# First chunk of an mLSTM cell with a feed-forward block: two pairs of up-blocks run in two halves of the batches, with attention of the other batches between them

## The chip, the cores and the metric

The kernel runs on one core of a Trainium2 chip. The metric is the device time of one launch in microseconds (us). The engines are named as in the profile: PE is TensorE (matmuls; PEld its weight loads), DVE is VectorE, ACT is ScalarE, POOL is GpSimd, SP is the engine whose queue issues all DMAs here.

## The reference

An mLSTM cell (batch 4, 8 heads, 768 steps, head size 40) is followed by a feed-forward block on 3072 tokens of width 320, with a hidden width of 2048.

```python
for t in range(S):
    m_new = np.maximum(f_gate[:, :, t] + m, i_gate[:, :, t])
    f_stab = np.exp(f_gate[:, :, t] + m - m_new)
    i_stab = np.exp(i_gate[:, :, t] - m_new)
    C = f_stab * C + i_stab * outer(v_t, k_t)      # per batch and head, 40x40
    n = f_stab * n + i_stab * k_t
    y[:, :, t] = sigmoid(o_gate[:, :, t]) * (C @ q_t) / np.maximum(np.abs(n @ q_t), 1.0)
...
x = y.transpose(0, 2, 1, 3).reshape(B * S, H * D)  # 3072 x 320
h = x @ w_in                                       # 320 x 2048
out = (h * sigmoid(1.702 * h)) @ w_out             # 2048 x 320
```

All of it is float32.

## The kernel before, in words

The 768 steps are worked off in six chunks (`w`) of 128. In a chunk the recurrence is written as masked attention, batch by batch (`b` = 0 to 3, eight heads each), plus, from the second chunk on, a term from the carried state. The functions that follow are named with their lines in the kernel before.

- `gates(w)` (L226): scans over the gates on DVE, which give the running maximum and what the decay weights need. For the first chunk POOL and DVE split the values into three bf16 parts; for later chunks the running maximum is stored to DRAM (`m_row`, L256) and `spread(w)` (L297) loads it back as a broadcast into `wt`.
- `transposes(w, b)` (L284): k and q with the head size on the partitions. In the first chunk PE does it (L294, eight matmuls a batch) and ACT copies the result (L295); later DVE does it (L288) out of `k_bl` and `q_bl`, which `load_blocks` fills. In the first chunk the tile `q_bl` holds q itself, under the name `q_st`.
- `weights(w, b)` (L304): the decay weights `wt`, in the first chunk by sixteen matmuls (L312, L313) and an Exp on ACT (L314), then a causal mask by a select on POOL (L321).
- `scores(w, b)` (L326): sixteen small matmuls (L331), multiplied with `wt` on DVE (L333).
- `values(w, b)` (L335): 32 small matmuls (L342) and a chain on DVE (L356 to L362) with the sigmoid of the output gate (written with Tanh) and the normalisation, which gives `y`; POOL copies 64 columns of it (L364).
- `seam(w, b)` (L366): three transposes of `y` on PE (L371), copied by ACT into `xT` (L372), the input of the feed-forward block, 512 columns wide: 128 for each batch.
- `up(w, j)` (L397): two pairs of up-blocks, that is, 4 x 128 hidden units. `full` (L407) multiplies the first 256 rows of `w_in`, `rest` (L413) the last 64; then GELU on ACT (L418). `down` (L429) multiplies with `w_out`.
- `carry(w, b)` (L374): the update of the carried state (POOL L378, PE L383, DVE L392 or L394).
- `convert(n)` (L212): the weights come as raw bits, in twenty pieces of 512 KB; each piece is worked over by two ACT instructions (L216, L217) and four DVE instructions (L218 to L223). Pieces 0 and 1 hold the rows 0 to 255 of `w_in` for the first four up-blocks, piece 2 the last 64 rows for the first eight (`w_in_x`), 3 and 4 the next four, and so on; pieces 10 to 19 are `w_out`. `fetch(n)` (L150) loads a piece. Pieces 0 to 5 lie in the six buffers of the pool `sp`, which pieces 10 to 15 use next; so the load of piece 10 waits for the conversion of piece 0, and so on to 15 and 5. The table `beside` says which pieces are converted and fetched with which pair of up-blocks, or down-block.
- `keep_busy(n)` (L174): n matmuls on a tile of zeros, 128x512 in bf16, whose result nobody reads (L176).

The order of the work is written out by hand: every engine executes its instructions in the order in which the program emits them, and waits, instruction by instruction, for the semaphores of what it needs. A PSUM pool of four buffers, `ps_a`, serves transposes, weights, scores, values and seam in turn; a second of four, `ps_m`, serves the up- and down-blocks (and the filler matmuls).

In the first chunk (L533 to L555) the order before is: `gates(0)` and `gates(1)`; then for each batch the transposes, the scores of the batch before it, the weights; pieces 0 and 1 are converted on the way; then POOL clears `state`, `q_bl` and `k_bl` (L541 to L543), and `columns(0)`, the values and the seams of the four batches follow, with fillers between. Only then does the loop over up-blocks start (L569), each block 512 columns wide. After the first pair of blocks come the load of the next output gate, `spread(1)` and `load_blocks(1)` (L580).

Of the kernel before, what the change touches and what calls it, by code (L numbers as in the profile page):

```python
# [8 lines left out]
FP = mybir.dt.float32  # L9
U32 = mybir.dt.uint32  # L10
BF = mybir.dt.bfloat16
AF = mybir.ActivationFunctionType
# [22 lines left out]
def kernel(  # L35
# [13 lines left out]
    B, H, S, D = q.shape  # L49
# [36 lines left out]
    eo = {}  # L86
# [4 lines left out]
    def load_gates(w):  # L91
        for dst, src in ((f_sb, f_gate), (i_sb, i_gate)):
            dst[w] = ld.tile([BH, L], FP, tag="fi", bufs=4, name="fi")
            nc.sync.dma_start(out=dst[w], in_=src[:, :, w * L:(w + 1) * L].rearrange("b h s -> (b h) s"))
# [7 lines left out]
            nc.sync.dma_start(out=dst[:, hs, 0:D],  # L102
                              in_=src[bs, :, w * L:(w + 1) * L, :].rearrange("b h s d -> s (b h) d"))

    def load_blocks(w):
        for dst, src in ((k_bl, k), (q_bl, q)):
            for two in range(2):
                for d in range(0, D, 32):
                    n = min(32, D - d)
                    r = two * 64 + d  # L110
                    for g in range(L // 32):
                        t = w * L + g * 32
                        nc.sync.dma_start(
                            out=dst[r:r + 32, :, g, 0:n],
                            in_=src[:, two:H:2, t:t + 32, d:d + n].rearrange("b j s d -> s (b j) d"))
# [34 lines left out]
    def fetch(n):  # L150
        pool = gp if 6 <= n < 10 else sp
        bits[n] = pool.tile([128, 512, 2], U32, tag="g", name="bits")
        for r, c, src in pieces[n][1]:
            nc.sync.dma_start(out=bits[n][r, c].rearrange("p a two -> p (a two)"), in_=src)

    load_gates(0)
    for b in range(B):
        load(0, "kq", slice(b, b + 1))
        if b == 1:
            load_gates(1)  # L160
        if 0 < b < 3:
            fetch(b - 1)
    for b in range(B):
        load(0, "vo", slice(b, b + 1))
    for n in range(2, 6):
        fetch(n)


# [5 lines left out]
    def keep_busy(n):  # L174
        for _ in range(n):
            T.matmul(p_idle, idle, idle.unsqueeze(1).to_broadcast([128, 4, 128]), start=True, stop=True)  # L176
# [217 lines left out]
                V.tensor_copy(out=state[r, ps, i, :], in_=pc[r])  # L394


    def up(w, j):  # L397


        x = xT[w].rearrange("p c b t -> p c (b t)")  # L400
        ph = {}

        def full(j, first):
            for c in range(2):
                for i in range(2):
                    f = 2 * j + i
                    T.matmul(ph[j][i], w_in_sb[:, c, f * 128:(f + 1) * 128], x[:, c, :], start=(first and c == 0),  # L407
                             stop=(not first and c == 1))

        def rest(j, first):  # L410
            for i in range(2):
                r = slice(i * 64, i * 64 + 64)
                T.matmul(ph[j][i], w_in_x[r, j, :], x[r, 2, :], start=first, stop=not first)  # L413

        def gelu(j):
            g = gs[w, j] = gp.tile([128, 2, W], FP, tag="g", name="g")
            for i in range(2):
                A.activation(out=g[:, i, :], in_=ph[j][i], func=AF.Gelu_apprx_sigmoid)  # L418

        for j, first in ((j, True), (j + 1, False)):  # L420
            ph[j] = [ps_m.tile([128, W], FP, tag="m", name="p_h") for _ in range(2)]
            if first:
                full(j, True)
            rest(j, not first)
            if not first:
                full(j, False)
            gelu(j)
# [94 lines left out]
            f(*args)  # L522


    gates(0)
    gates(1)
    for n in range(6, 10):
        fetch(n)
    for b in range(B + 1):
        if b < B:  # L530
            transposes(0, b)
        if b:
            scores(0, b - 1)  # L533
        if b < B:
            weights(0, b)
        if b:
            keep_busy(2)
        if 0 < b < 3:
            convert(b - 1)
    G.memset(v_st[:, :, D:D1], 1.0)  # L540
    G.memset(state, 0.0)  # L541
    G.memset(q_bl, 0.0)  # L542
    G.memset(k_bl, 0.0)  # L543
    columns(0)
    for b in range(B + 1):
        if b < B:
            hs = slice(b * H, (b + 1) * H)
            A.activation(out=eo[0][:, hs, :], in_=eo[0][:, hs, :], func=AF.Tanh, scale=0.5)
            values(0, b)
            keep_busy(2)  # L550
        else:
            keep_busy(3)
        if b:
            seam(0, b - 1)
    keep_busy(3)  # L555
    convert(2)


    beside = {0: ((3, 4, 5), range(10, 16)), 1: ((6, 7, 8), ()), 2: ((9, 10, 11), (16, 17)), 3: ((12, 13, 14), (18, 19)),
              4: ((15, 16), ()), 9: ((17,), ()), 12: ((18,), ()), 14: ((19,), ())}  # L560

    def weights_in(n):
# [6 lines left out]
    for w in range(NW):  # L569
        more = w + 1 < NW  # L570
        for j in range(NF // 2):
            if j % 2 == 0:
                if w == 0:
                    weights_in(j // 2)
                up(w, j)
            if j == 0 and more:
                load(w + 1, "o")
            if w == 0 and j == 0:
                spread(1)
                load_blocks(1)  # L580
            if w == 1 and j == 1:
                weight_sums()
            if more:
                if w and j == 0:
                    gates(w + 1)
                if j == 4:
                    load(w + 1, "v")
                if w and j == 4:
                    spread(w + 1)
                if j == 4:  # L590
                    load(w + 1, "k")
                if j < B:
                    carry(w, j)
                if 4 <= j < 6 if w else j == 7:
                    first = 2 * j - 8 if w else 0
                    transposes(w + 1, first)
                    transposes(w + 1, first + 1)
            if w and j >= 4:
                hidden_sums(w, (j - 4,), False)
                if j % 2:  # L600
                    hidden_sums(w, (j - 5, j - 4), True)
        side = attention(w + 1) if more else []
        if w == 0:

            blocks = [(lambda b=b, n=n: down(w, b, n)) for ns in ((0, 1), (2,), (3,)) for b in range(B) for n in ns]
            stops = (0, 1, 4, 7, 9, 11, 13, 15)
        else:
            blocks = down_fast(w, 0) + down_fast(w, 1)
            stops = (0, 1, 2, 4, 6, 8, 10, 12)
        for i, block in enumerate(blocks):  # L610
            if w == 0:
                weights_in(4 + i)
                if i in (6, 9):
                    transposes(1, i // 3)
            if w + 2 < NW and i == (0 if w else 9):
                load_gates(w + 2)
                load_blocks(w + 2)
            block()
            if i in stops and side:
                run(side.pop(0))  # L620
# [30 lines left out]
```

## Time and profile before

| | us |
|---|---|
| median of 9 runs | 524.09 |
| lowest, highest | 522.28, 526.94 |
| the profiled execution's own time | 524.12 |
| its span, first to last instruction | 522.4 |

| in the profiled execution | us after the start of the span |
|---|---|
| first transposes on PE | 5.13 |
| first up-block starts | 36.13 |
| first two pairs of up-blocks done, state update starts | 45.31 |
| first down-block starts | 74.05 |
| second chunk's first up-block starts | 123.11 |

A line of a timeline shows the start, the duration (for merged lines from the first start to the last end), the engine, the line of the kernel, the operation, the tiles (out <- in), the shape, the count, and in brackets the time that the engine had been idle before and who ended the wait. PE's records overlap, since matmuls are pipelined: two successive starts, not the durations, give the pace. The page gives busy shares, the chain of work that ended last, and the costliest groups.

### The profile page before, as it was taken

The numbers are of one execution on the slowest core, as the hardware profiler recorded it, in microseconds if no ns is written. First come the engines' busy times: TensorE is split into PE (matmuls) and PEld (weight loads), VectorE is DVE, ScalarE is ACT, GpSimd is POOL, SyncE is SP. The second block draws the span as 40 slices with busy tenths as digits, with TensorE's granted clock in tenths as the row PEclk, the third lists the DMA queues.
The fourth block names the chain that finished last, engine by engine and source line by source line (L and its number), as shares of the span: only waits on it lengthen the run. The fifth ranks groups of instructions, "written<-read, shape, count | busy, mean of one in ns | idle before, by whom it ended". The sixth has DMA issues, their size and how long they took to land.

```text
span 522.4 us, 9549 instructions
## 1 busy us (share of the span) xinstructions
PE 514.6 (98%) x3828; PEld 353.1 (68%) x3828; DVE 267.1 (51%) x603; ACT 169.0 (32%) x367; POOL 70.1 (13%) x104
## 2 busy tenths in 40 slices
PE   8999999999999999999999999999999999999997
PEld 5764447774447998445999544999643799744797
DVE  7769755874675454146445226564217455203511
ACT  3557456612223520322720212630221450032100
POOL 4341000112500212200112100020220021000000
PEclk9999999999999999999999999999999999999999
DMA  9979979267396200596300496500376000000000
GB/s 165 148 246 313 220 76 198 69 76 127 50 230 73 30 14 27 85 231 73 30 26 1 78 243 68 56 28 1 78 163 99 0 28 1 26 0 1 1 26 25
DMA packets 175884, 44.81 MB, mean 86 GB/s; under 512 B 164544, under 2 KB 170720, under 8 KB 175840
## 3 DMA queue, kind: packets, MB, share of 16 engines
q1 hardware_dynamic: 175840, 44.21, 44.8%
q8 instruction: 30, 0.49, 0.4%
q14 instruction: 14, 0.11, 0.1%
HBM read 40.17 MB, written 4.01 MB: 85 GB/s over the span
## 4 chain that ended last, share of the span: by engine, by line
PE 95%; POOL 2%; issue 1%; DVE 1%; ACT 0%; POOLq 0%; DVEq 0%
PE p_h L407 33%; PE p_out L488 30%; PE p_h L413 9%; PE p_out L434 7%; PE p_s L331 5%; PE p_o L342 4%; PE p_i L348 2%; PE p_x L371 1%; PE p_c L383 1%; PE p_t L294 1%; PE p_w L313 0%; PE p_w L312 0%; PE p_idle L176 0%; POOL q_bl L542 0%; POOL k_bl L543 0%
## 5 line engine op out<-in xcount | busy, mean ns | idle before, releaser
L407 PE MATMUL p_h<-xT,w_in_sb 128*128 128x512 f32 x384 | 175.1, 602 | 0.6 <-ACT xT L372 0.6
L407 PEld LDWEIGHTS p_h<-xT,w_in_sb 128*128 128x128 f32 x384 | 69.8, 190 | 92.6 <-issue 89.7
L418 ACT ACTIVATE g<-p_h 128x512 f32<-128x512 f32 x96 | 54.6, 596 | 135.4 <-PE p_h L413 73.5
L488 PE MATMUL p_out<-w_out_sb,g 128*128 128x160 f32 x480 | 71.3, 302 | 0.0
L488 PEld LDWEIGHTS p_out<-w_out_sb,g 128*128 128x128 f32 x480 | 66.8, 190 | 3.7 <-issue 2.4
L493 DVE TENSOR_TENSOR o_sb<-o_sb,p_out 128x160 f32<-128x160 f32 x70 | 21.4, 318 | 65.1 <-PE p_out L488 64.9
L321 POOL TENSOR_SCALAR_AFFINE_SELECT wt<-wt 128x1024 f32<-128x1024 f32 x24 | 26.2, 1093 | 199.7 <-ACT wt L318 186.9
L372 ACT COPY xT<-p_x 128x384 f32<-128x384 f32 x24 | 11.5, 479 | 120.5 <-PE p_x L371 120.5
L413 PE MATMUL p_h<-xT,w_in_x 64*128 64x512 f32 x192 | 48.4, 616 | 0.7 <-ACT g L418 0.7
L318 ACT ACTIVATE wt<-wt,cols 128x128 f32<-128x128 f32 x160 | 48.4, 392 | 0.0
L488 PE MATMUL p_out<-t,s 128*128 128x160 f32 x320 | 47.5, 301 | 0.0
L488 PEld LDWEIGHTS p_out<-t,s 128*128 128x128 f32 x320 | 44.3, 190 | 0.6
L472 DVE TENSOR_TENSOR s<-g 128x512 f32<-128x512 f32 x20 | 13.9, 693 | 54.0 <-ACT g L418 53.6
L333 DVE TENSOR_TENSOR wt<-p_s,wt 128x512 f32<-128x512 f32 x48 | 30.8, 684 | 17.1 <-POOL wt L321 14.9
L392 DVE TENSOR_TENSOR state<-p_c,state 40x164 f32<-40x164 f32 x32 | 10.4, 326 | 55.9 <-PE p_c L383 55.5
L413 PEld LDWEIGHTS p_h<-xT,w_in_x 64*128 64x128 f32 x192 | 16.7, 186 | 30.7 <-issue 27.3
L434 PE MATMUL p_out<-w_out_sb,g 128*128 128x320 f32 x128 | 36.2, 437 | 0.0
L434 PEld LDWEIGHTS p_out<-w_out_sb,g 128*128 128x128 f32 x128 | 23.8, 190 | 10.1 <-issue 0.5
L331 PE MATMUL p_s<-qT,kT 40*128 40x128 f32 x384 | 28.8, 291 | 0.9 <-DVE wt L333 0.9
L342 PEld LDWEIGHTS p_o<-v_st,wt 128*64 128x64 f32 x768 | 24.3, 138 | 4.6 <-issue 3.9
L331 PEld LDWEIGHTS p_s<-qT,kT 40*128 40x128 f32 x384 | 24.1, 193 | 4.6 <-DVE wt L333 1.4
L342 PE MATMUL p_o<-v_st,wt 128*64 128x41 f32 x768 | 27.2, 231 | 0.0
(114 smaller groups left out, 519.2 us busy)
## 6 DMA issues: line engine op xcount, KB each, us to landing
wt<-m_row SPq DMA_DIRECT2D x20, 512.0 KB, 6.8
bits<-in_moe_w_in_dram SPq DMA_DIRECT2D x8, 512.0 KB, 5.9
out_dram<-o_sb SPq DMA_DIRECT2D x24, 160.0 KB, 1.8
eo<-in_o_gate_dram SPq DMA_DIRECT2D x5, 640.0 KB, 5.4
v_st<-in_v_dram SPq DMA_DIRECT2D x5, 640.0 KB, 5.7
k_st<-in_k_dram SPq DMA_DIRECT2D x5, 640.0 KB, 8.4
bits<-in_moe_w_out_dram SPq DMA_DIRECT2D x8, 320.0 KB, 4.6
k_bl<-in_k_dram SPq DMA_DIRECT2D x40, 64.0 KB, 2.6
```

The costliest lines, as they stand in the source:

```text
L318: A.activation(out=x[:, h, :], in_=x[:, h, :], func=AF.Exp, scale=-1.0, bias=cols[w][:, b * H + h:b * H + h + 1])
L321: G.affine_select(out=x, in_=x, compare_op=OP.is_ge, fill=0.0, base=0, pattern=[[0, H], [1, L]], channel_multiplier=-1)
L331: T.matmul(pw[i][:, p, :], kT[w, b][r, p, :], qT[w, b][r, p, :], start=True, stop=True)
L333: V.tensor_tensor(out=wt[w, b][:, :, i, :], in0=pw[i], in1=wt[w, b][:, :, i, :], op=OP.mult)
L342: T.matmul(po[t, h, :], wt[w, b][:, p, i, t], v_st[:, b * H + h, :], start=True, stop=True)
L407: T.matmul(ph[j][i], w_in_sb[:, c, f * 128:(f + 1) * 128], x[:, c, :], start=(first and c == 0), stop=(not first and c == 1))
L413: T.matmul(ph[j][i], w_in_x[r, j, :], x[r, 2, :], start=first, stop=not first)
L418: A.activation(out=g[:, i, :], in_=ph[j][i], func=AF.Gelu_apprx_sigmoid)
L434: T.matmul(po, gs[w, f // 2][:, f % 2, b * L:(b + 1) * L], w_out_sb[:, f, :], start=(f == 0), stop=(f == NF - 1))
L472: V.tensor_tensor(out=s1, in0=a10, in1=a11, op=OP.add)
L488: T.matmul(po, a(f), b[:, f, :], start=(f == 0), stop=(f == NH - 1))
L493: V.tensor_tensor(out=dst, in0=x, in1=po, op=OP.add)
```

## The change

The first chunk gets another order. The loads are issued in the order in which the new order uses them: k and q of batches 0 and 1, the first weight piece, v and the output gate of batch 0, k and q of batch 2, and so on; the second chunk's gates are loaded after the first six pieces. Attention of the first two batches is finished first (their values and seams are run between transposes, scores and weights of batches 2 and 3). Then `up(0, 0)` takes a new argument: it allocates all four PSUM tiles of its two pairs, works on the columns of batches 0 and 1 (256 of 512), and between the parts of this half calls, in this order, scores of batch 3 and values of batch 2; values of batch 3; the seams of batches 2 and 3 and the conversion of pieces 3 and 4. Then the second half, the columns of batches 2 and 3, follows. The Tanh of the output gate becomes a function, `gate_out`. `gates(1)` runs after `up(0, 0)` and the conversion of piece 5, and `load_blocks(1)` is split in two, k before `spread(1)` and q after it. The three big clears of POOL are emitted after the weights of batch 3. Sixteen filler matmuls are left of thirty. The diff, without the parts that only rename:

```diff
-    load_gates(0)
-    for b in range(B):
-        load(0, "kq", slice(b, b + 1))
-        if b == 1:
-            load_gates(1)
-        if 0 < b < 3:
-            fetch(b - 1)
-    for b in range(B):
-        load(0, "vo", slice(b, b + 1))
-    for n in range(2, 6):
-        fetch(n)
+    load_gates(0)
+    for what, n in (("kq", 0), ("kq", 1), (fetch, 0), ("vo", 0), ("kq", 2), ("vo", 1), (fetch, 1), ("kq", 3), (fetch, 2),
+                    ("vo", 2), ("vo", 3), (fetch, 3), (fetch, 4), (fetch, 5)):
+        if what is fetch:
+            fetch(n)
+        else:
+            load(0, what, slice(n, n + 1))
+    load_gates(1)
+    for n in range(6, 10):
+        fetch(n)
...
+        if between:
+            for k in (j, j + 1):
+                ph[k] = [ps_m.tile([128, W], FP, tag="m", name="p_h") for _ in range(2)]
+            ts = slice(0, W // 2)
+            full(j, True)
+            between[0]()
+            rest(j, False)
+            rest(j + 1, True)
+            between[1]()
+            full(j + 1, False)
+            between[2]()
+            ts = slice(W // 2, W)
...
     gates(0)
-    gates(1)
-    for n in range(6, 10):
-        fetch(n)
-    for b in range(B + 1):
-        if b < B:
-            transposes(0, b)
-        if b:
-            scores(0, b - 1)
-        if b < B:
-            weights(0, b)
-        if b:
-            keep_busy(2)
-        if 0 < b < 3:
-            convert(b - 1)
-    G.memset(v_st[:, :, D:D1], 1.0)
+    transposes(0, 0)
+    weights(0, 0)
+    transposes(0, 1)
+    scores(0, 0)
+    weights(0, 1)
+    keep_busy(2)
+    convert(0)
+    scores(0, 1)
+    keep_busy(2)
+    gate_out(0)
+    transposes(0, 2)
+    values(0, 0)
+    weights(0, 2)
+    keep_busy(2)
+    gate_out(1)
+    convert(1)
+    values(0, 1)
+    scores(0, 2)
+    seam(0, 0)
+    transposes(0, 3)
+    weights(0, 3)
     G.memset(state, 0.0)
     G.memset(q_bl, 0.0)
     G.memset(k_bl, 0.0)
+    keep_busy(2)
+    seam(0, 1)
     columns(0)
-    for b in range(B + 1):
-        if b < B:
-            hs = slice(b * H, (b + 1) * H)
-            A.activation(out=eo[0][:, hs, :], in_=eo[0][:, hs, :], func=AF.Tanh, scale=0.5)
-            values(0, b)
-            keep_busy(2)
-        else:
-            keep_busy(3)
-        if b:
-            seam(0, b - 1)
-    keep_busy(3)
     convert(2)
+    gate_out(2)
+    gate_out(3)
...
-    beside = {0: ((3, 4, 5), range(10, 16)), ...
+    beside = {0: ((5,), range(10, 16)), ...
...
-                if w == 0:
-                    weights_in(j // 2)
-                up(w, j)
+                if w == 0 and j == 0:
+                    up(w, j, (lambda: (scores(0, 3), values(0, 2)), lambda: values(0, 3),
+                              lambda: (seam(0, 2), seam(0, 3), convert(3), convert(4))))
+                    weights_in(0)
+                else:
+                    if w == 0:
+                        weights_in(j // 2)
+                    up(w, j)
...
             if w == 0 and j == 0:
+                gates(1)
+                load_blocks(1, 0)
                 spread(1)
-                load_blocks(1)
+                load_blocks(1, 1)
```

The memset of the ones in `v_st` moves ahead of `gates(0)`.

## The prediction

> **What bounds the kernel now.** I read the page first (busy shares and the chain that ended last), then PE's timeline for the first 80 us, then those of DVE, ACT, POOL and the SP queue over the same stretch.
>
> ```profile
> PE 514.6 (98%) x3828; PEld 353.1 (68%) x3828; DVE 267.1 (51%) x603; ACT 169.0 (32%) x367; POOL 70.1 (13%) x104
> ...
> PE 95%; POOL 2%; issue 1%; DVE 1%; ACT 0%; POOLq 0%; DVEq 0%
> ```
>
> TensorE (PE) is the bound: 95% of the chain. The change touches only the first chunk, so the question is by how much PE reaches the end of the first two pairs of up-blocks (the L407 and L413 matmuls up to 45.31 us) earlier or later; whatever PE gains or loses there is carried to the end, provided DVE and the loads keep step.
>
> ```profile
> 22.96 0.60 PE L176 MATMUL p_idle<-idle 128*128 128x512 bf16 x2
> 24.44 1.16 PE L331 MATMUL p_s<-qT,kT 40*128 40x128 f32 x16 [0.88 <-DVE wt L333]
> ...
> 36.13 3.70 PE L407 MATMUL p_h<-xT,w_in_sb 128*128 128x512 f32 x8
> 39.76 1.99 PE L413 MATMUL p_h<-xT,w_in_x 64*128 64x512 f32 x8
> 41.68 3.70 PE L407 MATMUL p_h<-xT,w_in_sb 128*128 128x512 f32 x8
> 45.31 0.81 PE L383 MATMUL p_c<-vw,k_st 128*40 128x41 f32 x32
> ```
>
> The reader should see that both pairs take 45.31 - 36.13 = 9.2 us, that they begin only when all four batches' attention is done, and that PE waits little before (0.88 us here). Much of PE's time before 36 us is filler: the L176 matmuls.
>
> POOL matters too, because of what DVE does while POOL runs. Two places, the second as pieces of the chain:
>
> ```profile
> 1.31 0.74 POOL L199 MEMSET k_st<- 128x768 f32 x1
> 1.41 1.72 DVE L189 TENSOR_SCALAR pick<-ident 32x32 bf16<-32x32 f32 x3 [0.40 <-POOL ident masks.py:199]
> ...
> 1.99 0.74 POOL L199 MEMSET q_bl<- 128x768 f32 x1
> ```
>
> ```profile
> 1.41 1.35 DVE pick L189
> 2.77 0.17 DVE pick L189
> ```
>
> Equal instructions: the first takes 1.35 us, the next 0.17, and the first ends at 2.76, where POOL's two memsets end (1.99 + 0.74 = 2.73). DVE did not get in between the two memsets. The same with a select:
>
> ```profile
> 16.42 0.84 DVE L218 TENSOR_SCALAR w_in_sb<-w_in_sb 128x512 f32<-128x512 f32 x1 [1.66 <-ACT w_in_sb L216]
> ...
> 36.68 0.43 DVE L218 TENSOR_SCALAR w_in_x<-w_in_x 128x512 f32<-128x512 f32 x1 [1.86 <-ACT w_in_x L216]
> 37.14 0.43 DVE L219 TENSOR_SCALAR w_in_x<-w_in_x 128x512 uint32<-128x512 uint32 x1
> ```
>
> L218 needs 0.43 alone, and 0.84 when it starts inside POOL's select of 15.89 to 16.98. The memsets that the change moves (with one of `state`, 1.1 us, ahead of them):
>
> ```profile
> 26.10 1.81 POOL L542 MEMSET q_bl<- 128x2048 f32 x1
> 27.84 1.80 POOL L543 MEMSET k_bl<- 128x2048 f32 x1
> ```
>
> They follow each other without a gap, straight after the last select.
>
> [...] L189 and L218 (tensor_scalar) are held, while L356 to L360, which read PSUM, keep their 0.17 to 0.44 us during the memsets of 25 to 29.6 us. [...] Here 16 p_s take 2.08 us at 11.28 and 1.16 at 17.49, so the clock rose near 17 us in this execution; no fall is seen after it.
>
> **The change, step by step.** Letters per batch: T = eight L294, W = sixteen L312/L313, S = scores L331, V = values L342, X = seam L371. Prices at full clock from the timelines: PE T 1.0, W 0.9, S 1.09, V 1.06, X 0.33, two fillers 0.45. DVE: product after S 1.25 (L333 twice), chain after V 1.48 (27.33 to 28.81; p_o is free after 0.96), one convert 2.36 (36.68 to 39.04). ACT: copy 0.5 to 0.6, Exp 0.55, each half of a convert 0.57 (DVE can start after 0.65). POOL: select 1.05, the three memsets 1.1 + 1.75 + 1.75 = 4.6.
>
> *Removed:* 14 of 30 fillers, 14 x 0.21 = 3.0 us of PE. *Halved matmuls:* the first four up-blocks run as 256 columns twice. 160-column products (L488) and 320-column ones (L434) cost the same per column (L434: 32 in 8.81 us), so I price this at nothing; PE's work covers the 0.19 us weight loads. Bounds 0 to 0.3 us. *Load order:* in the record of before, 160 KB of k, q, v or o land about 1.1 us apart and a 512 KB piece 1.4 us after the one before; in the new order v0/o0 land near 12 us, k2/q2 14, k3/q3 20, v3/o3 26, each ahead of its use below. *Gates later:* 2.4 us of DVE (L231 to L268) leave 8.7 to 12, where DVE then idles, and come after the sixth convert; its two loads move behind the first six pieces in SP's queue, where nothing waits for them before 51 us, and its m_row store from ahead of piece 6 to behind piece 15 (costed below). The memset of v_st's ones (0.16 us) goes into POOL's 1.77 us of idleness ahead of L239.
>
> The walk in the changed order. Until 15.8 us PE does as before. S1 to 17.7, fillers 18.1, T2 19.1, V0 (after the kT copy) 19.4 to 20.5, W2 21.4, fillers 21.9, V1 22.9, S2 24.0, X0 24.35. DVE meanwhile: first convert 16.4 to 19.2, product 1 to 20.45, chain 0 20.6 to 22.1, second convert (ACT reaches it at 22.75) 23.4 to 25.8, chain 1 to 27.3, product 2 to 28.55. The q part of T3 takes the PSUM buffer of V1, free at 26.76: PE idles 1.4 + 0.5 us, T3 ends 27.4, W3 28.4 (behind the kT copy and product 2), fillers 28.85, X1 29.2, columns 29.4, first half of the first up-block 29.75 to 31.55, S3 32.65, V2 33.7.
>
> Next PE wants w_in_x, the third convert. ACT gets to it at 29.95 (its columns step waits for DVE's), so L218 is ready at 30.6. But POOL begins the select of batch 3 at 29.2 (end of its Exp) and has the three memsets right behind it: busy until 29.2 + 1.05 + 4.6 = 34.85. **Here the change adds a wait:** L218 is held as L189 was, and behind it on DVE stand the rest of the convert, product 3, chains 2 and 3. In the kernel before, no tensor_scalar ran beside those memsets. So: convert 34.85 to 37.2, product 3 38.45, chain 2 39.95, chain 3 41.45, POOL's y copy 41.7, X3 42.05, ACT's copy 42.55. PE: idle 33.7 to 37.2, rest-halves 38.2, V3 39.45, half of the second block 41.3, X2, X3, and the second half (4.6 us) from 42.6 to 47.2. Before: 45.3. **Loss 1.9 us.**
>
> What is late next: the converts 4 and 5 (DVE 43.15 to 47.9) are there when PE, after its two L383 groups, wants them at 47.95; the sixth waits on ACT behind the four GELUs, 49.05 to 51.4; gates to 53.8, state copies 55.1, then converts back to back: the fifteenth ends 77.7, where PE wants it at 77.65. PE runs 1.9 to 2.0 us behind the old timeline all the way. SP: piece 15 waits for the buffer of the sixth convert (51.4; before 46.1), then o_gate, m_row, k_bl (8.7 to 10), spread (2), q_bl (8.5 to 12.9): q_bl lands at 75 to 81 against
>
> ```profile
> 79.02 0.71 DVE L288 STREAM_TRANSPOSE qT<-q_bl 128x512 f32<-128x512 f32 x1 [4.79 <-DMA q_bl<-in_q_dram]
> ```
>
> and DVE has 0.5 us of slack behind it (product of batch 1 ends 100.3, V wants it at 100.83). With PE itself 1.9 late this hides, up to 81.4. Sum: 524.12 (span 522.4 and 1.7 around it) + 1.9 = **526.0 us**; that execution is 0.03 above the median of 524.09.
>
> **Rivals.** *(a) POOL doesn't hold L218* (the memsets only write, and L218 slips in). Then the third convert ends at 33.0 to 33.4, rest-halves follow V2 without a gap, chain 3 ends 37.7, the second half runs 38.9 to 43.5, and PE gains 1.8, of which DVE's fifteenth convert (74.1) leaves 1.6: 522.5 us. For it: the removed fillers; against it: L189. *(b) DVE gets in between memsets:* L218 after the first, L219 after the second (33.4), convert ends 35.3, second half 40.7 to 45.3: no change, 524.1. Against it: L189 waited through both. *(c) The clock:* [...] the 3.5 us gap at 33.7 drops it again (V3, rests and half block, 3.8 us, at double): about 528.5 in either mixture. No record of before shows such a drop. The bounds of the forecast itself: starts on ACT and DVE within 1.2 us either way. The forecast ends slower; (a) is the one on the other side, and it decides by one point: whether L218 of the third convert starts before 31.4 us of its timeline or only when the q_bl/k_bl memsets are over.
>
> **Chances.** Forecast 0.48, (a) 0.26, (b) 0.13, (c) 0.13. What a measurement of this kernel can tell from no change is about 0.3%, 1.6 us. The forecast lies just over that line and gives slower 0.33, same 0.13, faster 0.02; (a) gives faster 0.2, same 0.06; (b) same 0.08, faster 0.03, slower 0.02; (c) slower 0.12, same 0.01. Together faster 0.25, same 0.28, slower 0.47. Range from (a) to (c): 522.2 to 528.5; the forecast alone 524.8 to 527.2.
>
> **What would show it.** In the timeline after: L218 of w_in_x (third convert) lasting some 4 us and ending with the k_bl memset; a PE wait of 3 us or more before the rest-halves, released by DVE; the second half starting near 42.6. Wrong if that L218 takes 0.43, if the p_c group starts well before 45.3, or if p_s groups after 18 us still last 2 us (then the clock, (c)). A q_bl wait ending after 81.4 would make the loss larger by the excess.

## The result, and the profile after

| | before | after |
|---|---|---|
| median | 523.55 (32 runs, 521.29 to 526.94) | 531.49 (10 runs, 527.24 to 533.34) |
| ratio, 95% interval | | 1.0146 [1.0125, 1.0167] |
| profiled execution: own time, span | 524.12, 522.4 | 532.16, 530.5 |
| first (half) up-block starts | 36.13 | 30.86 |
| first two pairs of up-blocks done (p_c starts) | 45.31 | 51.09 |
| first down-block starts | 74.05 | 79.83 |
| q_bl's first transpose on DVE | 79.02 | 87.58 |
| copy of the second chunk's columns on DVE | 85.63 | 94.19 |
| second chunk's first up-block starts | 123.11 | 131.16 |

The change made the kernel 1.5% slower, four times as much as forecast. The last row holds all of it: what follows the second chunk's first up-block takes 399.3 us in every profile of this study (399.25 to 399.34 in 17 kernels), so nothing after it plays a part. An eleventh run of the changed kernel took 528.06 us and is not among the ten.

PE's timeline of the changed kernel, to be set against the one shown of the kernel before:

```profile
15.97 2.08 PE L332 MATMUL p_s<-qT,kT 40*128 40x128 f32 x16
...
30.86 1.99 PE L410 MATMUL p_h<-xT,w_in_sb 128*128 128x256 f32 x8 [0.48 <-ACT xT L373]
32.79 1.16 PE L332 MATMUL p_s<-qT,kT 40*128 40x128 f32 x16
33.88 1.13 PE L343 MATMUL p_o<-v_st,wt 128*64 128x41 f32 x32
38.12 2.08 PE L416 MATMUL p_h<-xT,w_in_x 64*128 64x256 f32 x8 [3.11 <-DVE w_in_x L224]
40.13 1.93 PE L343 MATMUL p_o<-v_st,wt 128*64 128x41 f32 x32
41.99 2.91 PE L410 MATMUL p_h<-xT,w_in_sb 128*128 128x256 f32 x8
44.74 0.82 PE L372 MATMUL p_x<-ident,y 128*128 128x128 f32 x6
46.18 1.99 PE L410 MATMUL p_h<-xT,w_in_sb 128*128 128x256 f32 x8 [0.62 <-ACT xT L373]
```

Three things are to be seen. PE waits 3.11 us for the third convert, as forecast. Behind the wait the same instructions take nearly twice as long as ahead of it: 32 p_o 1.93 instead of 1.13 us, the rest-halves 2.08 where the second half's take 1.13. The trace records the granted clock at 0.50 from 37.05 to 43.88 us. And the p_s of batch 1 still take 2.08 us at 15.97, so the clock also rose late. The table of stretches (start:end, length, then busy time of PE, PEld, DVE, ACT, POOL with counts, the granted PE clock, the DMA share, GB/s) shows the fall directly. (Its record begins with the first rise: before that its column reads 1.00, also where the p_s still take 2.08 us, so a first rise is read from the pace or from the record's first entry, 19.98 us here.)

```profile
30.00:35.00 5.00, 4.52 (x60) 3.59 (x58) 3.50 (x3) 2.74 (x7) 4.76 (x4) 1.00 0.82 271
35.00:40.00 5.00, 1.89 (x10) 1.19 (x8) 4.76 (x9) 0.00 (x0) 1.23 (x1) 0.71 0.72 219
40.00:45.00 5.00, 5.00 (x45) 4.28 (x44) 2.00 (x7) 0.00 (x0) 1.51 (x4) 0.61 0.98 356
```

Where the 3.11 us come from stands in DVE's and POOL's timelines:

```profile
31.66 2.83 DVE L219 TENSOR_SCALAR w_in_x<-w_in_x 128x512 f32<-128x512 f32 x1 [1.05 <-ACT w_in_x L217]
34.52 1.99 DVE L220 TENSOR_SCALAR w_in_x<-w_in_x 128x512 uint32<-128x512 uint32 x1
```

```profile
31.27 1.19 POOL L568 MEMSET state<- 128x1312 f32 x1
32.40 1.81 POOL L569 MEMSET q_bl<- 128x2048 f32 x1
34.15 2.08 POOL L570 MEMSET k_bl<- 128x2048 f32 x1
```

Each of the two DVE instructions needs 0.43 us alone. The first lasts until 34.49, just past the end of the q_bl memset (34.21), the second until 36.51, just past that of the k_bl memset (36.23). The last view is DVE's wait for q_bl (the brackets name the transfer of a weight piece, which landed at about the same time; the instruction reads q_bl alone, whose last load SP had issued by 85.38):

```profile
87.58 0.71 DVE L289 STREAM_TRANSPOSE qT<-q_bl 128x512 f32<-128x512 f32 x1 [5.09 <-DMA bits<-in_moe_w_out_dram]
...
94.19 0.19 DVE L279 COPY cols<-p_cols 128x32 f32<-128x32 f32 x1
```

It comes 8.56 us later than before, while PE is only 5.78 later at p_c and at the first down-block.

### The profile page after: what moved, and what is told of

Its sections match the earlier page's. It is cut to its first block, busy times and chain, and to the rows that moved or that the text cites. A ratio compares the mean times of both kernels' runs of the same rounds, so it can differ in the third digit from the quotient of the medians.

```text
span 530.5 us, 9566 instructions
## 1 busy us (share of the span) xinstructions
PE 516.9 (97%) x3838; PEld 358.4 (68%) x3838; DVE 270.2 (51%) x603; ACT 169.0 (32%) x367; POOL 70.4 (13%) x104
## 4 chain that ended last, share of the span: by engine, by line
PE 85%; SPq 5%; issue 5%; DMA 4%; DVE 1%; ACT 0%; POOL 0%; DVEq 0%; POOLq 0%
PE p_h L410 31%; PE p_out L504 30%; PE p_h L416 9%; PE p_o L343 4%; PE p_s L332 4%; SPq L102 3%; PE p_out L450 3%; PE p_i L349 2%; SPq L155 2%; DMA bits<-in_moe_w_in_dram 2%; PE p_c L384 1%; PE p_x L372 1%; DMA wt<-m_row 1%; DMA bits<-in_moe_w_out_dram 1%; ACT xT L373 0%
## 5 line engine op out<-in xcount | busy, mean ns | idle before, releaser
L410 PE MATMUL p_h<-xT,w_in_sb 128*128 128x512 f32 (+1 forms) x400 | 176.6, 588 | 1.7 <-ACT xT L373 1.7
L410 PEld LDWEIGHTS p_h<-xT,w_in_sb 128*128 128x128 f32 x400 | 73.3, 191 | 91.4 <-issue 86.9
L416 PE MATMUL p_h<-xT,w_in_x 64*128 64x512 f32 (+1 forms) x200 | 49.7, 610 | 3.8 <-DVE w_in_x L224 3.1
L334 DVE TENSOR_TENSOR wt<-p_s,wt 128x512 f32<-128x512 f32 x48 | 30.8, 683 | 20.2 <-POOL wt L322 14.9
L416 PEld LDWEIGHTS p_h<-xT,w_in_x 64*128 64x128 f32 x200 | 17.9, 191 | 33.3 <-issue 26.9
L343 PEld LDWEIGHTS p_o<-v_st,wt 128*64 128x64 f32 x768 | 25.4, 141 | 6.0 <-issue 4.7
L343 PE MATMUL p_o<-v_st,wt 128*64 128x41 f32 x768 | 28.4, 235 | 0.7 <-ACT xT L373 0.3
```

Of the source, the lines that this page charges most:

```text
L334: V.tensor_tensor(out=wt[w, b][:, :, i, :], in0=pw[i], in1=wt[w, b][:, :, i, :], op=OP.mult)
L343: T.matmul(po[t, h, :], wt[w, b][:, p, i, t], v_st[:, b * H + h, :], start=True, stop=True)
L410: T.matmul(ph[j][i][:, ts], w_in_sb[:, c, f * 128:(f + 1) * 128], x[:, c, ts], start=(first and c == 0), stop=(not first and c == 1))
L416: T.matmul(ph[j][i][:, ts], w_in_x[r, j, :], x[r, 2, ts], start=first, stop=not first)
```

## The experiments

The theory after the result: three costs lie in a row. The hold of the convert by the clears, the fall of the clock in the gap that the hold makes, and a late q_bl behind the late sixth convert. The rivals: the late rise of the clock at the start makes most of it; or PE's 5.8 us are the whole, and q_bl merely follows. The groups of runs come from different chips, so versions of different groups are compared by their ratios to the kernel before. e3 asked in addition whether the order of the second chunk's gates is behind q_bl's delay.

**e1, e2, e3, e4** (one chip; the kernel before had 523.23 there, 12 runs). e1 takes the clears away from the convert:

```diff
     gates(0)
+    G.memset(state, 0.0)
+    G.memset(k_bl, 0.0)
     transposes(0, 0)
...
-    G.memset(state, 0.0)
-    G.memset(q_bl, 0.0)
-    G.memset(k_bl, 0.0)
...
+                G.memset(q_bl, 0.0)
                 load_blocks(1, 1)
```

> The changed kernel with POOL's three clears moved: state and k_bl right after gates(0), where POOL and DVE idle, q_bl after the first two pairs of up-blocks. Theory (POOL's clears hold DVE's tensor_scalar of the third convert, which starves PE, which drops the clock): that convert's two tensor_scalar take 0.43 us each in place of 2.83 and 1.99, PE's wait of 3.1 us before the rest-halves is under 0.6, the p_s and p_o groups after it keep the full pace, the first p_c group starts near 45 in place of 51.1, and the time falls by some 7 us to 523.5 to 525. Rival (the halves, the new load order or the missing fillers cost the time by themselves): PE's wait only moves to another DVE or DMA, p_c stays beyond 48 and the time stays above 528.

e2 leaves the clears and fills the gap with fillers on a PSUM tile of their own:

```diff
-up(w, j, (lambda: (scores(0, 3), values(0, 2)), ...
+up(w, j, (lambda: (scores(0, 3), values(0, 2), stay_busy(14)), ...
```

> The changed kernel with 14 filler matmuls (3 us at full clock) in the gap before the rest-halves, written to a PSUM buffer of their own turn. The hold stays. Theory (the gap's own length costs 2 us, the dropped clock behind it another 3): L220 stays at 2 us, the rest-halves start at 38.1 as before, but then take 1.1 and the next p_o group 1.1, the half block 2.0, so the first p_c starts near 48 and the time falls by about 3 us to 528.5. Rival (the slow groups are slow by their own waits, not by the clock): nothing changes, 531.5.

e3 leaves the clears, loads the second chunk's gates after k and q of batch 1 and runs them early:

```diff
     gates(0)
+    gates(1)
...
-                gates(1)
                 load_blocks(1, 0)
```

> The changed kernel with the next chunk's gates, and their two loads, back at the start. Theory (behind the first part, 2.3 us are lost because the SP queue brings q_bl late: m_row waits for the late gates and the converts behind them are 2.4 us later): p_c stays at 51.1, m_row no longer takes 3.7 us of the SP queue behind piece 15, q_bl lands near 84 in place of 87.6, the second chunk starts 2 us earlier, time near 529.3. Rival (q_bl is late because piece 15 waits for the late sixth convert alone): q_bl lands within 1 us of 87.6, time 531.5.

e4 is e1 and e3 together:

> Both edits, the clears away and the gates early. Theory: p_c near 45, then no wait for q_bl beyond that of the kernel before, 522 to 523.5, level with the kernel before or up to 1.5 us faster. Rival (the halves cost by themselves): above 526.

Measured: e1 526.3, ratio to before 1.0068 [1.0046, 1.0091]; e2 528.97, 1.0111 [1.0085, 1.0138]; e3 528.74, 1.0099 [1.0061, 1.0136]; e4 524.65, 1.0035 [1.0015, 1.0054]. PE in e2, after the same V2 as above:

```profile
35.02 3.19 PE L544 MATMUL p_stay<-idle 128*128 128x512 bf16 x14
38.20 1.13 PE L416 MATMUL p_h<-xT,w_in_x 64*128 64x256 f32 x8
39.26 1.15 PE L343 MATMUL p_o<-v_st,wt 128*64 128x41 f32 x32
40.34 1.99 PE L410 MATMUL p_h<-xT,w_in_sb 128*128 128x256 f32 x8
```

The clock is at full speed throughout (two stretches of the table of e2):

```profile
35.00:40.00 5.00, 5.00 (x51) 2.72 (x48) 4.76 (x9) 0.00 (x0) 1.31 (x1) 1.00 0.64 193
40.00:45.00 5.00, 4.38 (x35) 3.69 (x31) 2.78 (x9) 2.30 (x5) 1.87 (x4) 1.00 1.01 363
```

The gap is as long (3.19 us), PE does nothing useful in it, and everything behind it is fast again: p_c 48.52 instead of 51.09. So the fall of the clock is shown, and priced at 2.57 us in the profile. The ratios give 1.8 us (1.0146 and 1.0111), with intervals that just overlap. In e4 the two DVE instructions take 0.43 us each, PE does not wait, and p_c stands at 45.34:

```profile
31.75 0.43 DVE L221 TENSOR_SCALAR w_in_x<-w_in_x 128x512 f32<-128x512 f32 x1 [1.05 <-ACT w_in_x L219]
32.21 0.43 DVE L222 TENSOR_SCALAR w_in_x<-w_in_x 128x512 uint32<-128x512 uint32 x1
```

The changed kernel (after), e2 and e4 start their first half block at the same moment (30.86, 30.94, 30.95), so they form a ladder: 51.09, 48.52, 45.34; the last rung, 3.18 us, is the hold. e4's PE is where the kernel before has it (45.31), and yet e4's second chunk starts at 124.98 instead of 123.11, with q_bl's transposes at 81.41 instead of 79.02. e1 shows the same more sharply. In its profile, the fastest of its four runs, the clock had risen by 6.4 us, p_c comes at 42.03, 3.3 us ahead of the kernel before, and the second chunk starts at 122.95: the lead is lost, because q_bl's transposes start at 79.38 after a wait of 5.73. Expected were 523.5 to 525 for e1 and 522 to 523.5 for e4; both came out too slow, so something besides PE had to be priced. e3's p_c (47.64) is not a gain of the gates: its clock had risen by 6.3 us too, and its DVE instruction was held 4.13 us in one piece. Nor is the order of the gates behind q_bl's delay: from the issue of the output gate's load to q_bl's first transpose it takes 30.8 us in e3 and 31.2 in the changed kernel.

**e5 to e8** (before: 522.67, 57 runs). The theory now says that q_bl's arrival sets the second chunk. e5 is e4 with the sixth convert ahead of the GELUs:

```diff
-lambda: (seam(0, 2), seam(0, 3), convert(3), convert(4))))
+lambda: (seam(0, 2), seam(0, 3), convert(3), convert(4), convert(5))))
...
-    beside = {0: ((5,), range(10, 16)), ...
+    beside = {0: ((), range(10, 16)), ...
```

> e4 with the sixth weight conversion (piece 5) emitted beside conversions 3 and 4, ahead of the GELUs, so that the load of piece 15 no longer waits in SP's queue. Theory (what is left of the loss is the arrival of q_bl, which lands about 29 us after piece 15 is through SP's queue): the fourteen transfers of pieces 10 to 15 take 8 to 9 us of issue instead of 12.3, q_bl's transposes start at about 79.4 instead of 81.4, and the median is about 523. Rival (what is left is the clock[...]): the p_c group stays where it is and the median stays at 524.6.

e6 goes on from e5:

```diff
-    beside = {0: ((), range(10, 16)), ...
+    beside = {0: ((), range(10, 15)), ...
...
-            if j == 0 and more:
+            if w and j == 0 and more:
                 load(w + 1, "o")
...
                 load_blocks(1, 1)
+                load(1, "o")
+                fetch(15)
```

> e5 with the second chunk's output gate and piece 15 loaded behind q_bl instead of ahead of it (about 1.2 MB less in front of q_bl). Theory: the transfers in front of q_bl set its arrival, so the transposes of q_bl start about 3 us earlier than in e5, near 76, and PE's lead, where an execution has one, is kept: median about 521 to 522. Rival (q_bl's own 128-byte rows set its arrival, not what is in front): transposes stay near 79, median as in e5.

e7 (from e6) and e8 (from the kernel before) have one edit, at the start:

```diff
-    keep_busy(8)
+    keep_busy(11)
```

> e6 with eleven filler matmuls at the start instead of eight, so that PE is busy without a gap from 1.06 us through the first transposes. Theory [...]: 16 p_s take 1.16 us already at about 10 us, the first half block starts near 27.7 in most executions, median 1 to 2 us under e6, about 520. Rival (the start has no influence on it): as e6.

> The kernel before with eleven filler matmuls at the start instead of eight, nothing else. Theory: the clock rises early here too and the first up-block starts some 2 us before 36.1, but q_bl still arrives at about 79, so the median stays within 0.5 us of 523.2. Rival (PE alone bounds the kernel before): median 521 or less. If the clock still rises near 17 us, neither is tested.

Measured: e5 526.01, 1.0056 [1.0040, 1.0071]; e6 525.09, 1.0029 [1.0008, 1.0051]; e7 525.09, 1.0035 [1.0021, 1.0049]; e8 522.37, 0.9993 [0.9981, 1.0006].

e8 is the control. Three more fillers, and in this profile the clock has risen by the first p_s; PE starts the up-blocks 3.3 us earlier than before, and gets nothing for it (PE, then DVE):

```profile
9.67 1.16 PE L331 MATMUL p_s<-qT,kT 40*128 40x128 f32 x16
...
32.80 3.70 PE L407 MATMUL p_h<-xT,w_in_sb 128*128 128x512 f32 x8
...
41.98 0.81 PE L383 MATMUL p_c<-vw,k_st 128*40 128x41 f32 x32
...
123.31 3.70 PE L407 MATMUL p_h<-xT,w_in_sb 128*128 128x512 f32 x8 [0.57 <-ACT xT L372]
```

```profile
79.73 0.71 DVE L288 STREAM_TRANSPOSE qT<-q_bl 128x512 f32<-128x512 f32 x1 [7.36 <-DMA q_bl<-in_q_dram]
```

The median agrees: no gain that can be told, as expected. e5 tested nothing: the sixth convert ended at 49.94 as in e4, since DVE itself starts the fourth only when ACT has copied the seams (2.2 us idle). e6 brought q_bl's transposes to 76.37 as expected, and p_c stood at 40.68, since its clock had risen by 5.3 us; but it missed its 521 to 522. The columns came at 87.51: converts 15 and 16 stand ahead of that copy on DVE, and now piece 15 was the late one. PE then waited 3.60 us for batch 0's product, and its clock fell again (the next 16 p_s took 2.08 us). e7 did not become faster than e6 either: its early clock was lost when the p_s of batch 1 waited 3.21 us for DVE. There the clears at their new place held another tensor_scalar, one of `gates(0)`, for 2.98 us instead of 0.28, and `gates(1)` followed before batch 0's product.

**e9 to e12** (before: 523.05, 55 runs). e9 is e8 with converts 15 and 16 moved behind the columns; e10 is the changed kernel with only the way to q_bl shortened; e11 joins it all; e12 is e4 with converts 3 to 5 ahead of the seams.

```diff
-              4: ((15, 16), ()), 9: ((17,), ()), ...
+              6: ((15, 16), ()), 9: ((17,), ()), ...
```

> e8 (the kernel before with eleven start fillers) with the conversions of pieces 15 and 16 moved from ahead of the first down-block to ahead of the third, so that DVE copies the second chunk's columns straight after the four transposes of k_bl and q_bl. Theory (q_bl, then two conversions of 2.35 us each, then the columns on DVE are the path into the second chunk, and PE's early lead is lost there): the columns copy follows q_bl's arrival by 2 us instead of 6.6, the second chunk's first up-block starts 2 to 3 us earlier than 123.3 in an execution in which the clock rises early, median 520 to 521. Rival (PE is the bound there): as e8, 522.4.

e10 has this edit, the output gate and piece 15 as in e6, and

```diff
+                load_blocks(1)
                 gates(1)
-                load_blocks(1, 0)
                 spread(1)
-                load_blocks(1, 1)
```

> The changed kernel with its clears, its gap and its clock untouched; only the way to q_bl is shortened: k_bl and q_bl are loaded straight after piece 14, ahead of the second chunk's gates, m_row, output gate and piece 15, and the conversions of pieces 15 and 16 come after the columns. Theory (of the 8.05 us at the second chunk 5.8 are PE's own and 2.3 are q_bl's): p_c stays near 51, the second chunk starts near 128.7 instead of 131.2, median about 529. Rival (PE's 5.8 us alone make the loss): as the changed kernel, 531.5.

> e6 (clears and gates early, output gate and piece 15 behind q_bl) with the columns ahead of conversions 15 and 16, as in e9, and conversions 3, 4 and 5 emitted right after the values of batch 3, ahead of the seams of batches 2 and 3. Theory: both waits that swallowed PE's lead are gone; columns near 79 to 80; second chunk's first up-block at 119 to 121.5 by the clock; median 519 to 521.5, under both kernels. Rival (a third wait stands behind, for instance the conversion of piece 17 or the product of batch 0): 523 or more.

e12, and e11 too, have

```diff
-lambda: values(0, 3),
-lambda: (seam(0, 2), seam(0, 3), convert(3), convert(4), convert(5))))
+lambda: (values(0, 3), convert(3), convert(4), convert(5)),
+lambda: (seam(0, 2), seam(0, 3))))
```

> e4 (clears and gates early) with conversions 3, 4 and 5 emitted right after the values of batch 3, ahead of the seams of batches 2 and 3, instead of behind them. In e5 the sixth conversion did not move, because DVE was the late one (it idles 2.2 us for ACT, which stands behind the xT copies). Theory: the sixth conversion ends at 47 instead of 49.9, piece 15 is issued by 48, q_bl's transposes start near 79, second chunk at about 122.8, median 522.5 to 523.3. Rival (q_bl's arrival isn't tied to the sixth conversion): as e4 and e5, 524.7 to 526.

Measured: e9 522.26, 0.9987 [0.9973, 1.0000]; e10 530.4, 1.0109 [1.0063, 1.0155]; e11 522.53, 0.9987 [0.9970, 1.0004]; e12 525.18, 1.0037 [1.0024, 1.0051].

e10 came between its theory (529) and its rival (531.5), and its interval overlaps that of the changed kernel; e9 and e11 missed theirs (520 to 521, 519 to 521.5). With these the second chunk's start can be written down. PE's own way from the first down-block takes 49.06 us (before). The other way, from the copy of the columns on DVE over ACT, DVE and PE, takes 36.97 us (after). The later of the two ends wins:

| kernel | first (half) block | p_c | q_bl transposed from | first down + 49.06 | columns + 36.97 | second chunk |
|---|---|---|---|---|---|---|
| before | 36.13 | 45.31 | 79.02 | **123.11** | 122.60 | 123.11 |
| after | 30.86 | 51.09 | 87.58 | 128.89 | **131.16** | 131.16 |
| e1 | 27.64 | 42.03 | 79.38 | 119.82 | **122.95** | 122.95 |
| e2 | 30.94 | 48.52 | 85.01 | 126.32 | **128.59** | 128.58 |
| e3 | 27.72 | 47.64 | 83.65 | 125.43 | **127.23** | 127.22 |
| e4 | 30.95 | 45.34 | 81.41 | 123.14 | **124.99** | 124.98 |
| e5 | 30.95 | 45.34 | 81.75 | 123.13 | **125.33** | 125.33 |
| e6 | 26.29 | 40.68 | 76.37 | 118.47 | 124.48 | 125.88 |
| e7 | 31.34 | 45.73 | 76.54 | 123.53 | **124.71** | 124.71 |
| e8 | 32.80 | 41.98 | 79.73 | 119.78 | **123.31** | 123.31 |
| e9 | 32.80 | 41.98 | 78.06 | 119.78 | 116.96 | 121.39 |
| e10 | 31.03 | 51.56 | 82.89 | **129.35** | 121.75 | 129.36 |
| e11 | 29.34 | 43.72 | 76.50 | **121.52** | 115.40 | 121.53 |
| e12 | 29.33 | 43.72 | 81.68 | 121.51 | **125.26** | 125.26 |
| e13 | 26.26 | 46.95 | 83.60 | 124.74 | **127.18** | 127.17 |
| e14 | 26.70 | 47.49 | 84.16 | 125.28 | **127.74** | 127.73 |
| e15 | 28.94 | 45.34 | 74.97 | **123.13** | 113.87 | 123.14 |

The two constants were read from before and after alone; the sum then gives ten of the other kernels where DVE ends last and three where PE does, to 0.01 us. The table explains one profiled execution of each kernel. Executions differ: the runs of the kernel before spread over more than 5 us, and e8's profile is the slowest of its 20 runs, so what a version is worth is said by the medians. The two exceptions have their reasons in sight: e6 lost 1.4 us more to the fall of the clock, and in e9 neither is last, since the product of batch 0 now stands behind converts 15 and 16 on DVE (it starts at 90.23, and PE waits 0.96 and 0.37 us). e10 shows it for the changed kernel, in its profile: with q_bl out of the way and PE no better (p_c 51.56), the second chunk starts 1.80 us earlier, at PE's own bound. Two things were moved there, q_bl's load (transposed 4.69 us earlier) and converts 15 and 16, which stood between q_bl and the columns (6.61 us from one to the other before, 1.89 in e10). By the sum either alone would have brought the columns below PE's bound; neither was run alone on the changed kernel.

```profile
PE 85%; SPq 5%; issue 5%; DMA 4%; DVE 1%; ACT 0%; POOL 0%; DVEq 0%; POOLq 0%
```

```profile
PE 95%; DVE 2%; ACT 1%; POOL 1%; issue 0%; ACTq 0%; POOLq 0%; DVEq 0%
```

The first is the chain of the changed kernel, the second that of e10: the SP queue and the DMAs, which stood on the chain with 5 and 4%, are gone from it. The first chain does not name q_bl (it runs through loads of `wt` and of weight pieces); q_bl is named by DVE's wait and by the sum.

e12 refutes part of the theory. Its sixth convert ends at 47.40 instead of 49.95 and the loads of pieces 10 to 15 take 8.32 us instead of 12.26, but q_bl comes no earlier (81.68 against 81.41). While the sixth convert holds up SP's queue, q_bl follows it; once it doesn't, the transfers ahead of q_bl fill the time (in e6, with 1.2 MB fewer of them, it came at 76.37). From the issue of the output gate's load to q_bl's first transpose it takes 30.9 us before, 31.2 after, 30.6 in e4, 32.5 in e12. Why e12's took 1.9 us longer than e4's stays open.

**e13 to e15** (before: 524.10, 15 runs). They ask how much of the loss belongs to the moment at which the clock rises. e13 is the changed kernel with `keep_busy(11)` in the first place, e14 with `transposes(0, 2)` ahead of `scores(0, 1)`:

```diff
     convert(0)
+    transposes(0, 2)
     scores(0, 1)
     keep_busy(2)
     gate_out(0)
-    transposes(0, 2)
     values(0, 0)
```

e15 is e11 with eleven fillers, `gates(1)` after the scores of batch 1 and the clear of k_bl after the values of batch 2:

```diff
-    gates(1)
-    G.memset(k_bl, 0.0)
...
     scores(0, 1)
+    gates(1)
...
-lambda: (scores(0, 3), values(0, 2)), ...
+lambda: (scores(0, 3), values(0, 2), G.memset(k_bl, 0.0)), ...
```

> The changed kernel with eleven start fillers instead of eight, nothing else. Theory [...]: first half block near 27.7, p_c near 47.6 as in e3 instead of 51.1, hold and fall of the clock in the gap unchanged, second chunk near 127.5, median about 528. Rival (the fillers have no part in it): as the changed kernel, 531.5.

> The changed kernel with the transposes of batch 2 ahead of the scores of batch 1, as the kernel before has them. Theory of the prediction's rival (c) [...]: the 16 p_s of batch 1 take 1.16 us instead of 2.08, first half block about 1 us earlier, near 29.8, median about 530.4. Rival (it is chance by execution): median 531.5 and the same spread of 6 us.

> e11 with eleven start fillers; DVE's gates of the second chunk after the scores of batch 1 (in e7 they waited for their load with product 0 behind them), and POOL's clear of k_bl after the values of batch 2. Theory: the clock rises early in most executions, p_c near 40.7, PE alone sets the second chunk's start (first down-block + 49.07), near 118.6, median about 519.5, below both kernels. Rival (the clock's rise stays as spread as in e11): 522.

Measured: e13 528.88, 1.0095 [1.0072, 1.0119]; e14 529.22, 1.0104 [1.0078, 1.0131]; e15 523.17, 0.9988 [0.9974, 1.0002]. With eleven fillers the clock had risen by 7 us in all five profiles (e7, e8, e9, e13, e15); with eight it had in seven of twelve, and in three of these it was down again by 8 us (e11, e12) or 9.5 (e10). (Read from the pace: the W matmuls of batch 0 follow each other in 0.055 us where the clock is up and in 0.107 where it is not. e10's first rise is read from the mean granted clock of its profile, 0.981 against 0.994 of the changed kernel.) In e14's it had risen by 6.31 us (the transposes there take 0.63 us), ahead of the place that was changed, so its profile says nothing on that order. Its ratio is under the changed kernel's by 2.2 us, from four runs and with intervals that just overlap. The clock records of the other kernels say more: the kernel before, with T2 in that place, rose at 17.24 us, and the five profiles with S1 there and a late clock (after, e2, e4, e5, and e10 for the second time) at 20.0 to 20.8. That speaks for a later rise with S1 in T2's place, on one profile of the kernel before; it is not shown. e13 shows what the moment is worth: an early clock makes the changed kernel some 2.6 us faster and does not cure it; its L219 is held for 4.57 us, and PE waits 3.64. e15 missed: its clock rose early and fell again at about 23 us (granted 0.73 from 22 to 24 us, 0.50 to 32), and the first half block took 3.78 us instead of 1.99. No version beats the kernel before by more than can be told; e8, e9, e11 and e15 equal it.

## Why the prediction was right or wrong

*The hold* (the forecast's one point) was right in its effect. L218 of the third convert, now L219, was held to the end of the q_bl memset, and the instruction behind it, now L220, to the end of the k_bl memset; PE's wait was 3.11 us where 3.5 were forecast, and without the hold (e4 against e2) p_c is 3.18 earlier. So DVE got in once between two memsets, which is rival (b)'s mechanism; it gained nothing, since the second of the two instructions still had to wait for the last memset. e3 and e13 show the hold in one piece, as forecast. Rival (a) is refuted. ("No tensor_scalar ran beside those memsets" in the kernel before is too strong: L356, whose input p_o lies in PSUM, is one, started inside them at 27.33 and 28.93, and took 0.17 us each time.)

*The walk up to the first half block* had 29.75; measured were 30.86. "Until 15.8 us PE does as before" held; what failed is "S1 to 17.7", which takes the clock to rise near 17 as before: in the profile it rose at 19.98, and S1 ended at 18.05. Its moment varies from one execution to the next (27.6 to 31.0 us for this half block in e1, e3, e2 and e10, with the same PE instructions ahead of it), so one profile could not give it.

*The rest-halves, V3 and the half block* were priced at full clock, 37.2 to 42.6 with the seams; they took 38.12 to 46.18, 2.7 us more. The drop stood in rival (c) and was given 0.13, with "No record of before shows such a drop" against it. A record without a gap of 3 us can't speak against that; e2 shows that the drop follows from the gap, and all seven waits of 2.8 us or more (2.84 to 3.66) that PE had in the first 140 us of these 17 profiles brought half clock with them (six while they lasted, that of e6 some 1.8 us after its end). By these seven, the drop belonged in a forecast that had a gap of 3.5 us. Rival (c)'s own figure was also too low: 1.9 and 3.8 us on top of 524.1 make 529.8, not "about 528.5".

*Halved matmuls* were priced at nothing, 0 to 0.3 us. The second half takes 4.91 us at full clock (46.18 to 51.09), half of the whole 4.59 (36.13 to 45.31): 0.3 for each half, so some 0.6 in all (an estimate from this one half). 160 and 320 columns had cost the same per column (0.136 and 0.269 us from start to start in the kernel before); 256 and 512 do not (eight take 1.93 and 3.63 us to the start of the next group).

*"With PE itself 1.9 late this hides, up to 81.4"* failed: nothing was hidden. Its criterion was right, the slack of 0.5 us is the difference of the two bounds in the table's first line (123.11 and 122.60). The arrival was mis-sized: 75 to 81 was pieced together from the shortest and longest times of k_bl, spread and q_bl (m_row, listed without a price, took 3.71 us on SP), where the record of before has the whole stretch, 48.11 to 79.02, 30.9 us. That, set behind the forecast's own end of the sixth convert (51.4), gives 82.3 and a loss already beyond PE's; with the measured end (55.47) it gives the 87.58 within 1.3 us.

*The sum* was 1.9; measured were 8.05 in the profile: 5.78 of PE and 2.27 of q_bl beyond it. Of the 6.1 us that were missing, 1.1 came ahead of the first half block, 2.7 from the drop behind the gap, 2.3 from q_bl. In the steps of the ladder, at equal rise of the clock: 2.58 the fallen clock (131.16 to 128.58), 3.60 the hold and the gates (to 124.98), 1.87 the way to q_bl (to 123.11).

*What bounds the kernel.* The first step read "PE 95%" of the chain and concluded that whatever PE gains in the first chunk is carried to the end, "provided DVE and the loads keep step". They don't: the profiled execution of the kernel before stands 0.5 us from a second bound, so a gain of PE above 0.5 us could not reach the end by itself (e1 and e8: 3.3 us ahead at p_c, 0.2 at most at the second chunk), while every loss could. Rival (a)'s 522.5, with its gain of 1.6 us, was out of reach for that reason alone. What the reordering was worth on PE can be read from profiles whose clock stayed up from an early rise to p_c: 40.68 in e6, 41.98 in e8 and e9. The interleaved order without its hold is 1.3 us faster on PE than the old one. (e1's 42.03 does not speak against that: its clock was at half from about 23.3 to 26.7 us, 0.83 granted over 20 to 30.)

## What to carry to other kernels

A share of 95% on the chain says which engine ended last, not by how much: before a gain on it is counted, find the next path into the same point and its distance (here 0.5 us, at a load that is wanted some 30 us after the place of the change). Price a chain of transfers by its whole measured stretch, from the instruction that frees it to the one that uses it, and not by its pieces. And where a change opens a gap on PE, count the gap twice, once as time and once as what the instructions behind it lose at half clock (here 3.11 us and 2.57 us).

## What the runs showed of the hardware

The moment at which the clock rises differs from one execution to the next. With eight fillers of 3.6 us in front, the first four transposes, near 5.1 us, already take 0.63 us in e11 and e12, where those of before and after take 1.09; in e5 the rise came as late as about 20.4 us (the transposes at 19.75 take 0.92 us instead of 1.06). PE was busy nearly throughout (8.0 of the first 10 us and all of the next 10, in before as in after). With three more fillers the rise came early in all five profiles.

The traces record the moments at which the granted clock changed. In those of before and after every stretch between two changes is a whole multiple of 3.41 us: 505.17 us before (148 steps), 17.07, 6.83 and 488.11 us after (5, 2 and 143). In the changed kernel the clock was full from 19.98 to 37.05, then half to 43.88. So the gap cost two steps of half clock: PE was busy for 40% of the step that ended at 37.05 and, the gap still open at its start, for 69% of the next. The wait of 3.11 us is shorter than a step, and in e15 the clock fell at about 22.9 behind waits of 0.67 and 0.57 us, PE having been busy for 64% of the 3.41 us before. In e1, e3, e11 and e12 it fell at 23 to 25 us (the transposes of q of batch 3 take 0.96 to 1.04 us), behind a wait of 1.13 or 1.14; behind the same wait of 1.13 it did not fall in e13, where they take 0.66. The columns are those of the stretches above, for e15:

```profile
20.00:22.00 2.00, 1.12 (x11) 0.51 (x7) 1.90 (x6) 0.17 (x1) 0.95 (x2) 1.00 0.16 45
22.00:24.00 2.00, 0.96 (x6) 0.73 (x7) 1.86 (x2) 0.90 (x2) 0.73 (x1) 0.73 0.39 100
24.00:26.00 2.00, 1.80 (x14) 1.53 (x13) 1.90 (x7) 0.59 (x1) 0.24 (x1) 0.50 0.93 177
```

In the first two stretches PE (the first time behind the length) was busy for about half. Its busy share does not decide alone: the changed kernel's PE had no wait from 7.86 us on, and yet its 16 p_s took 2.08 us at 11.28 and again at 15.97, and the clock rose at 19.98; and in e6, behind the wait of 3.60 us, 28 p_o at 92.89 still took 1.02 us (32 take 1.13 at full clock), and only the 16 p_s at 94.73 took 2.08. Whether the kind of matmul counts was not shown. e10 speaks for it: its clock rose again at about 20.75 (the transposes at 19.75 take 1.06 us, 32 p_o at 20.74 1.13), so a step ended near 17.3 (an estimate, 3.41 us earlier), and with S1 in T2's place that step brought no rise, where the kernel before rose at 17.24. What counts stays open.

The third convert's first DVE instruction, 0.43 us long in e4, lasted to the end of the second of POOL's three clears in after (2.83 us, to 34.49; the clear ended at 34.21) and took as long in e2 and e10 (2.82 and 2.83 us). In e3 and e13 it lasted past the third (4.13 us to 32.64, the clear to 32.35; 4.57 us to 31.63, the clear to 31.36), and in e14 it took 4.57 us too. What decides between the two was not settled.
